# A fused linear-attention and MLP kernel: exponentials kept in head order with a GpSimd copy of their last rows, and polynomials divided by their leading coefficients

## The chip, the cores and the metric

The kernel runs on one core of a Trainium2 chip. The metric is the device time of one execution in microseconds (us). Before the change it is 695.95 us, the median of 3 runs (695.08 to 697.68). The engines are called TensorE (PE in the profile; PEld are its weight loads), VectorE (DVE), ScalarE (ACT), GpSimd (POOL) and SyncE (SP, which issues every DMA of this path).

## The reference, cut to what matters

Three parts follow one another on 3072 tokens (4 batches of 768, 8 heads of 48):

```
S_t = a_t * S_(t-1) + k_t v_t^T       a complex, |a| cut at 0.999, one factor for each of 48 rows
y_t = Re(q_t S_t)                     -> x [3072, 384]
h   = x @ w_in                        [3072, 2048]
P   = a0 + a1 h + a2 h^2 + a3 h^3
Q   = 1 + |b0| |h| + |b1| h^2
out = (P / (Q + 1e-6)) @ w_out        [3072, 384]
```

A third part (a gated set of experts) only touches tokens whose product with `w_skip` is positive.

## The kernel before, in words

**Tiling.** The 3072 tokens are 24 chunks of 128; two chunks are a unit `u`, so there are 12 units. For the attention part each chunk gets running sums over its 128 tokens, made on TensorE by a triangular matrix: of the logarithm of |a| (`mm2`, L501) and of its angle (`mm1`, L479). Two exponentials of the first sum, exp(z) into `r1` (L505) and exp(-z) into `r2` (L506), are multiplied by q and k (`qrkr`, L513) and then by cosines and sines (`prods`, L523) to give `qt` and `kt`. TensorE transposes these (`xpose`, L539), multiplies them to scores (L557), ScalarE copies the scores to `pT` (L564), GpSimd clears their upper triangle (L566), and TensorE makes y from them and from the carried state (L582, L584). The state is updated by L603 and L610 and, in chunks that are not the last of a batch, multiplied by the chunk's total decay `dec`, which is the last row (partition 127) of `r1`, moved by two small DMAs onto 96 partitions (L510).

**Layout of r1.** In the kernel before, `r1` is a view of the tile `r1t`, which holds for each token 48 rows of 8 heads: `r1t = [128, 2, 48, 8]`, `r1 = r1t.rearrange("p c d h -> p c h d")`. The row of partition 127 is then already in the order in which the DMA into `dec` wants it. Everything else that writes or reads `r1` does so by heads, with steps of 8 elements: the exponential L505, the product with q (L516, L517) and the product with the cosines (L528). `r2` lies in the order of heads, and its operations (L506, L519, L528) are otherwise the same.

**The MLP.** Each of 96 steps (12 units of 8) takes 256 of the 2048 hidden columns for 256 tokens. `G1` (L670, 18 matmuls) makes h in a PSUM tile `hb`; the weights and x are split into a high and a low part, hence three products. Then nine operations work on 128x512 elements: a1 = Square(s3 h + c), a2 = Abs(s1 h), a3 = Square(a2 + t), a4 = Ln(a3 + q0) and a5 = Exp(-a4), on ScalarE; d1 to d4 on VectorE, of which d1 and d3 make P by Horner's rule in squares and d2 and d4 refine the reciprocal. `gh` and `gl` (L701, L703) split the result, and `G2` (L714, 12 matmuls) multiplies it by w_out into `ob`. s3, s1, c, t, k, q0, p0 and sg are columns of the small tile `cf`, made once by `coefs2` (L267): square roots of |a3| and |b1| by Ln and Exp on ScalarE and one Newton step, then c, t, k and q0 from them. An activation with `scale=fine["s3"]` reads the scale from a column of `cf`, one value for each partition; a `scale` that is a number is part of the instruction.

**The order of the work.** All of this is listed as tasks with costs, and `Plan.order` (L61) simulates the engines and writes the order of each engine's instructions out once. Tasks with more than one option (for instance `gh` on VectorE or ScalarE) are placed by that simulation. `PP` (L158) holds its parameters: `NO` names options that a task may not take, `T0` and `P` give the due times of the MLP's steps, `X1`, `E0` and `E1` those of `xhi` and `xlo` (L638), which split x for G1. Each engine then runs its list strictly in order, SP's DMAs too. `late=True` tasks get their ranks by another slack.

Of the kernel before, what the change touches and what calls it, by code (L numbers as in the profile page):

```python
# [29 lines left out]
class Plan:  # L30
# [30 lines left out]
    def order(self, slack, bias, ahead, hold, cold, only):  # L61
# [93 lines left out]
        self.span = now  # L155
        self.log = out
        return [o[2] for o in out]
PP = dict(NO={'kr': ('ACT', 'POOL'), 'gl': ('ACT', 'POOL'), 'S2': ('POOL',), 'wy': ('DVE', 'POOL'), 'e4': ('ACT',), 'ev': ('DVE', 'POOL'), 'msk': ('DVE', 'POOL'), 'xabs': ('DVE',), 'cadd8': ('DVE',), 'xpe': ('DVE',), 'xlo': ('ACT', 'POOL'), 'gh': ('POOL',), 'yev': ('DVE',)}, E0=-28.045, E1=-18.577, TC=40, WS=(0, 1, 2, 3, 4, 5, 0, 1, 1, 0, 1, 2, 2, 1, 2, 2), HO={('d2b', 'ACT'): 0.925, ('msk', 'ACT'): 0, 'DVE': 0, 'POOL': 8.743}, DW=86.219, WL=9, P=6.132, LAG2=4.681, SL={'ACT': 0.3, 'DVE': 2.523, 'POOL': 0.621, 'SP': 0.41, 'PE': 3.069, '2': 2.741}, X1=25.038, T0=82.051, NZ=2, NH=3, BI={'DVE': 2.383, 'POOL': 14.689})  # L158


def main_part(tc, ctx, q, k, v, a_re, a_im, w_in, w_out, moe_a, moe_b, w_skip, out, keep):
# [15 lines left out]
    def T(name, shape, dt=F32):  # L177
        return sb.tile(shape, dt, name=name)
# [88 lines left out]
    def coefs2():  # L267

        v = nc.vector
        root, ct, p = cf[:, 0:2], cf[:, 2:4], cf[:, 6:9]
        mag, pair, half, inv, top, sq, x = (cf[:, i:i + 2] for i in (12, 14, 16, 18, 20, 22, 24))
        F = NU + 1
        v.tensor_scalar(out=abcoef.bitcast(I32), in0=ar_bc[:, 4:6].bitcast(I32), scalar1=0x7FFFFFFF,
                        scalar2=None, op0=ALU.bitwise_and)
        v.tensor_scalar(out=mag.bitcast(I32), in0=ar_bc[:, 3:6:2].bitcast(I32), scalar1=0x7FFFFFFF,
                        scalar2=None, op0=ALU.bitwise_and)
        v.reciprocal(out=x, in_=mag)
        v.tensor_scalar(out=rsum[:, F:F + 2], in0=x, scalar1=2.0 ** -60, scalar2=None, op0=ALU.mult)  # L280
        v.tensor_scalar(out=rsum[:, F + 2:F + 4], in0=mag, scalar1=2.0 ** -60, scalar2=None, op0=ALU.mult)
        v.tensor_scalar(out=mag, in0=mag, scalar1=2.0 ** -60, scalar2=2.0 ** 60, op0=ALU.max, op1=ALU.min)
# [3 lines left out]
        v.tensor_tensor(out=x, in0=mag, in1=inv, op=ALU.mult)  # L286
        v.tensor_tensor(out=x, in0=x, in1=half, op=ALU.subtract)
        v.scalar_tensor_tensor(out=root, in0=x, scalar=0.5, in1=half, op0=ALU.mult, op1=ALU.add)
        v.reciprocal(out=inv, in_=root)
        v.tensor_scalar(out=cf[:, 10:11], in0=ar_bc[:, 3:4], scalar1=0.0, scalar2=2.0, op0=ALU.is_ge, op1=ALU.mult)  # L290
        v.tensor_scalar(out=cf[:, 10:11], in0=cf[:, 10:11], scalar1=-1.0, scalar2=None, op0=ALU.add)
        v.tensor_scalar(out=fine["sg"], in0=cf[:, 10:11], scalar1=-1.0, scalar2=None, op0=ALU.mult)
        v.tensor_scalar(out=p, in0=ar_bc[:, 0:3], scalar1=cf[:, 10:11], scalar2=None, op0=ALU.mult)
        v.tensor_copy(pair[:, 0:1], cf[:, 8:9])
        v.tensor_copy(pair[:, 1:2], abcoef[:, 0:1])
        v.scalar_tensor_tensor(out=ct, in0=pair, scalar=0.5, in1=inv, op0=ALU.mult, op1=ALU.mult)
        v.tensor_tensor(out=sq, in0=ct, in1=ct, op=ALU.mult)
        v.tensor_tensor(out=fine["k"], in0=cf[:, 7:8], in1=sq[:, 0:1], op=ALU.subtract)
        v.tensor_scalar(out=fine["q0"], in0=sq[:, 1:2], scalar1=-1.0, scalar2=QEPS, op0=ALU.mult, op1=ALU.add)
        v.tensor_scalar(out=x.bitcast(I32), in0=cf[:, 6:8].bitcast(I32), scalar1=0x7FFFFFFF, scalar2=None,  # L300
                        op0=ALU.bitwise_and)
        v.tensor_tensor(out=top[:, 0:1], in0=x[:, 0:1], in1=x[:, 1:2], op=ALU.max)
        v.tensor_scalar(out=top[:, 0:1], in0=top[:, 0:1], scalar1=1e-30, scalar2=WELL, op0=ALU.max, op1=ALU.mult)
        nc.vector.memset(top[:, 1:2], WELL)
        v.reciprocal(out=top, in_=top)
        v.tensor_tensor(out=rsum[:, F + 4:F + 6], in0=sq, in1=top, op=ALU.mult)

    def lnexp():
        nc.scalar.preload_act_table_set("natural_log_exp_and_others")  # L309

    def dma(*prs):
        def f():
            for o, i in prs:
# [145 lines left out]
    def cums(u, c):  # L459
# [196 lines left out]
    def step(s):  # L656
# [511 lines left out]
```

## Time and profile before

| | |
|---|---|
| median of 3 runs | 695.95 us (695.08 to 697.68) |
| the profiled execution | 693.37 us |
| its span, first to last instruction | 691.6 us |
| mean granted TensorE clock | 0.982 |
| instructions | 12738 |

The profiled execution lies 2.6 us below the median of the three runs. Between its span and its time lie 1.8 us. Busy times of an engine are unions of its instructions' records; a matmul's record is longer than its turn in the array, since matmuls overlap.

### The profile page before, as it was taken

The page shows a single profiled execution, that of the slowest core. Times are in us where ns is not written, and L with a number is a line of the kernel's source. Part 1 is how long each engine was busy: PE and PEld are TensorE (multiplying, and loading weights), DVE is VectorE, ACT ScalarE, POOL GpSimd, SP SyncE. Part 2 cuts the span into 40 slices and gives each one's busy share as a digit, 9 for nine tenths or more (in the row PEclk, how much of TensorE's full clock was granted, in tenths as well). Part 3 has the DMA queues.
Part 4 walks back from the last instruction along what each step waited for, and adds up shares of the span by engine and source line. Part 5 has one row for each costly group of instructions (what it writes and reads, how often), then busy time and mean ns, then how long its engine had stood idle before and what let it go on. Part 6 is the DMA issues. An engine that isn't in the chain of part 4 may idle for free.

```text
span 691.6 us, 12738 instructions
## 1 busy us (share of the span) xinstructions
PE 628.6 (91%) x4772; PEld 584.3 (84%) x4772; DVE 621.1 (90%) x1020; ACT 624.9 (90%) x1022; POOL 50.9 (7%) x73
## 2 busy tenths in 40 slices
PE   0477699899999999999999999999999999999994
PEld 0154689799988999999999999999989999899993
DVE  6899999999989998988989989988998988869992
ACT  5789999999999999998999998998999989968781
POOL 2024101010010010010010010010010010000000
PEclk9999799999999999999999999999999999999997
DMA  7734333132102202202102211212112110000000
GB/s 242 260 137 144 89 101 102 50 94 84 46 22 66 60 15 72 58 16 84 47 15 73 58 27 61 58 29 71 47 38 59 49 26 17 1 11 19 13 13 29
DMA packets 52137, 43.30 MB, mean 63 GB/s; under 512 B 31200, under 2 KB 48992, under 8 KB 52064
## 3 DMA queue, kind: packets, MB, share of 16 engines
q1 hardware_dynamic: 52064, 42.38, 20.3%
q8 instruction: 39, 0.64, 0.4%
q14 instruction: 34, 0.28, 0.1%
HBM read 36.38 MB, written 4.72 MB: 59 GB/s over the span
## 4 chain that ended last, share of the span: by engine, by line
PE 47%; ACT 25%; DVE 18%; issue 5%; DMA 2%; SPq 1%; DVEq 0%; ACTq 0%
PE hb L670 15%; PE ob L714 14%; ACT wk L318 9%; PE zb L557 5%; PE zb L539 5%; DVE wk L324 3%; PE zy L582 3%; PE zb L603 2%; ACT tb L318 2%; ACT r1t L505 2%; PE zy L584 2%; DVE qt L321 1%; DVE gl L700 1%; ACT L309 1%; ACT hb L318 1%
## 5 line engine op out<-in xcount | busy, mean ns | idle before, releaser
L670 PE MATMUL hb<-xh,wih 128*128 128x256 f32 x576 | 174.0, 302 | 8.7 <-DVE wk L324 6.7
L670 PE MATMUL hb<-xl,wih 128*128 128x256 f32 x576 | 164.1, 285 | 0.4 <-DVE xl L635 0.4
L670 PE MATMUL hb<-xh,wil 128*128 128x256 f32 x576 | 163.8, 284 | 0.0
L324 DVE SCALAR_TENSOR_TENSOR wk<-wk,cf,hb 128x512 f32<-128x512 f32 x192 | 141.9, 744 | 18.0 <-ACT wk L318 8.4
L318 ACT ACTIVATE wk<-hb,cf 128x512 f32<-128x512 f32 x192 | 134.2, 733 | 20.1 <-PE hb L670 19.7
L318 ACT ACTIVATE wk<-wk,cf 128x512 f32<-128x512 f32 x192 | 139.7, 728 | 0.7
L714 PE MATMUL ob<-woh,gh 128*128 128x384 f32 x384 | 137.6, 358 | 0.0
L714 PE MATMUL ob<-wol,gh 128*128 128x384 f32 x384 | 130.4, 340 | 0.0
L714 PE MATMUL ob<-woh,gl 128*128 128x384 f32 x384 | 130.1, 339 | 0.0
L670 PEld LDWEIGHTS hb<-xh,wih 128*128 128x128 f32 x576 | 110.6, 192 | 14.2 <-DVE wk L324 7.8
L670 PEld LDWEIGHTS hb<-xl,wih 128*128 128x128 f32 x576 | 110.9, 193 | 3.6 <-DVE xl L635 1.2
L670 PEld LDWEIGHTS hb<-xh,wil 128*128 128x128 f32 x576 | 110.8, 192 | 0.0
L566 POOL TENSOR_SCALAR_AFFINE_SELECT pT<-pT 128x512 f32<-128x512 f32 x48 | 38.1, 795 | 544.4 <-ACT pT L564 544.1
L700 DVE TENSOR_TENSOR gl<-wk,gh 128x512 fp32r<-128x512 f32 x96 | 67.5, 703 | 9.3 <-ACT gh L693 4.9
L714 PEld LDWEIGHTS ob<-woh,gh 128*128 128x128 f32 x384 | 72.7, 189 | 2.8 <-issue 1.4
L714 PEld LDWEIGHTS ob<-wol,gh 128*128 128x128 f32 x384 | 72.7, 189 | 1.5
L714 PEld LDWEIGHTS ob<-woh,gl 128*128 128x128 f32 x384 | 72.5, 189 | 0.0
L324 DVE SCALAR_TENSOR_TENSOR hb<-wk,cf,hb 128x512 f32<-128x512 f32 x96 | 72.0, 750 | 0.0
L324 DVE SCALAR_TENSOR_TENSOR wk<-wk,hb 128x512 f32<-128x512 f32 x96 | 65.7, 684 | 1.2
L318 ACT ACTIVATE hb<-wk 128x512 f32<-128x512 f32 x96 | 58.0, 604 | 2.2 <-DVE wk L324 1.3
L557 PE MATMUL zb<-qT,kT 96*128 96x128 f32 x384 | 51.5, 286 | 2.0 <-ACT qT L545 0.7
L557 PEld LDWEIGHTS zb<-qT,kT 96*128 96x128 f32 x384 | 47.5, 197 | 4.1 <-ACT kT L545 1.7
(160 smaller groups left out, 1073.5 us busy)
## 6 DMA issues: line engine op xcount, KB each, us to landing
wk<-in_moe_w_in_dram SPq DMA_DIRECT2D x8, 768.0 KB
ar<-in_a_re_dram SPq DMA_DIRECT2D x24, 192.0 KB
ai<-in_a_im_dram SPq DMA_DIRECT2D x24, 192.0 KB
qraw<-in_q_dram SPq DMA_DIRECT2D x24, 192.0 KB
kraw<-in_k_dram SPq DMA_DIRECT2D x24, 192.0 KB
vb<-in_v_dram SPq DMA_DIRECT2D x24, 192.0 KB
out_dram<-x2b SPq DMA_DIRECT2D x24, 192.0 KB
xl<-in_moe_w_out_dram SPq DMA_DIRECT2D x5, 384.0 KB
```

Of the source, the lines that this page charges most:

```text
L318: return ("ACT", cost, lambda: nc.scalar.activation(out=out, in_=in_, func=func, **kw))
L324: return ("DVE", cost, lambda: nc.vector.scalar_tensor_tensor(out=out, in0=in0, scalar=scalar, in1=in1, op0=op0, op1=op1, **kw), both)
L505: nc.scalar.activation(out=r1[:, c], in_=z.rearrange("p (h d) -> p h d", h=8), func=AF.Exp)
L539: nc.tensor.transpose(z[0:96, i, :], src[:, 4 * hf + i].rearrange("p z d -> p (z d)"), ident)
L557: nc.tensor.matmul(z[:, i, :], lhsT=kT[hf][:, i, :], rhs=qT[hf][:, i, :], start=True, stop=True)
L566: pl.add([("POOL", 0.6, lambda: nc.gpsimd.affine_select(out=pT[hf], in_=pT[hf], pattern=[[0, 4], [1, 128]], base=0, channel_multiplier=-1, ...
L582: nc.tensor.matmul(dst, lhsT=vt[:, h, :], rhs=pT[hf][:, i, :], start=True, stop=first)
L584: nc.tensor.matmul(dst, lhsT=state[:, h, :], rhs=qT[hf][:, i, :], start=False, stop=True)
L603: nc.tensor.matmul(z[:, h, :], lhsT=ktc[:, h].rearrange("p z d -> p (z d)"), rhs=vt[:, h, 0:48], start=True, stop=True)
L670: nc.tensor.matmul(h[:, i * 256:i * 256 + 256], lhsT=w[:, j, fs], rhs=x[:, j, :], start=(n == 0), stop=(n == 8))
L700: eng[e].tensor_tensor(out=ghl("gl", s), in0=uu, in1=ghl("gh", s).bitcast(F32), op=ALU.subtract)
L714: nc.tensor.matmul(o, lhsT=a[:, sl], rhs=w[:, f, :], start=(f == 0 and n == 0), stop=(f == NF - 1 and n == 2))
```

## The change

The tile `r1` is now `[128, 2, 8, 48]`, in the order of heads like `r2`, and L505 writes it flat. A new tile `last` of `[128, 48, 8]` takes, by a GpSimd `tensor_copy`, the partitions 96 to 127 of `r1` in the other order, and the two DMAs into `dec` read partition 127 of `last`. There is one `last` for all chunks; 20 of the 24 chunks make the copy.

The polynomials are divided by their leading coefficients: P by a3, Q by |b1|. So a1 is Square(h + c) and a2 is Abs(h), both without a scale read from `cf`, and a2 no longer reads `cf` at all; a3, a4, a5 and d1 to d4 keep their operations. The factor a3/|b1| goes into `sg`, which multiplied the result before too. `coefs2` no longer takes square roots: it has 22 small VectorE instructions and none on ScalarE, where it had 27 (a memset among them) and 2, and it no longer waits for `lnexp`, the load of the table for Ln and Exp.

The planner's costs of the touched tasks and its parameters `PP` are changed. In `NO`, `S2` may now go to GpSimd, `whi` (the high halves of the weights) may no longer go there, and `xhi` may no longer go to VectorE. The other limits have the same effect as before.

```diff
-PP = dict(NO={..., 'S2': ('POOL',), ..., 'msk': ('DVE', 'POOL'), ...}, E0=-28.045, E1=-18.577, ..., HO={..., 'POOL': 8.743}, DW=86.219, WL=9, P=6.132, LAG2=4.681, SL={'ACT': 0.3, 'DVE': 2.523, 'POOL': 0.621, 'SP': 0.41, 'PE': 3.069, '2': 2.741}, X1=25.038, T0=82.051, ..., BI={'DVE': 2.383, 'POOL': 14.689})
+PP = dict(NO={..., 'msk': ('DVE',), 'xhi': ('DVE',), 'whi': ('POOL',)}, E0=-21.161, E1=-11.963, ..., HO={..., 'POOL': 12.521}, DW=90.883, WL=8, P=6.022, LAG2=4.584, SL={'ACT': 0.3, 'DVE': 2.523, 'POOL': 0.529, 'SP': 0.926, 'PE': 3.069, '2': 2.738}, X1=18.065, T0=86.304, ..., BI={'DVE': 5.938, 'POOL': 10.587})
-    r1t = T("r1t", [128, 2, 48, 8])
-    r1 = r1t.rearrange("p c d h -> p c h d")
+    r1 = T("r1", [128, 2, 8, 48])
+    last = T("last", [128, 48, 8])
...
+        v.tensor_copy(pair[:, 0:1], ar_bc[:, 3:4])
+        v.tensor_copy(pair[:, 1:2], abcoef[:, 1:2])
+        v.reciprocal(out=inv, in_=pair)
...
-        nc.scalar.activation(out=half, in_=mag, func=AF.Ln)
-        nc.scalar.activation(out=half, in_=half, func=AF.Exp, scale=0.5)
-        v.reciprocal(out=inv, in_=half)
...
+        v.scalar_tensor_tensor(out=fine["sg"], in0=ar_bc[:, 3:4], scalar=-1.0, in1=inv[:, 1:2], op0=ALU.mult, op1=ALU.mult)
...
-            nc.scalar.activation(out=r1[:, c], in_=z.rearrange("p (h d) -> p h d", h=8), func=AF.Exp)
+            nc.scalar.activation(out=r1[:, c].rearrange(flat), in_=z, func=AF.Exp)
...
-        pl.add([("ACT", 0.8, ex)], reads=[tl], writes=[f"r1{c}", f"r2{c}"], free=tl, name=f"exp{ci}")
+        pl.add([("ACT", 0.95, ex)], reads=[tl], writes=[f"r1{c}", f"r2{c}"], free=tl, name=f"exp{ci}")
         if ci % CPB != CPB - 1:
-            pl.add(dma(*[(dec[ci % ND][48 * z:48 * z + 48, :], r1t[127:128, c])
-                         for z in range(2)]), reads=[f"r1{c}"], writes=[("dec", ci % ND)], name=f"dec{ci}")
+            pl.add([("POOL", 0.5, lambda: nc.gpsimd.tensor_copy(last[96:128], r1[96:128, c].rearrange("p h d -> p d h")))],
+                   reads=[f"r1{c}"], writes=["last"], name="last")
+            pl.add(dma(*[(dec[ci % ND][48 * z:48 * z + 48, :], last[127:128]) for z in range(2)]), reads=["last"], writes=[("dec", ci % ND)], name=f"dec{ci}")
...
-        pl.add([act(0.66, uu, h, AF.Square, scale=fine["s3"], bias=fine["c"])], reads=hks + ["cf"], writes=[U], name="a1", late=True)
-        pl.add([act(0.57, qa, h, AF.Abs, scale=fine["s1"])], reads=hks + ["cf"], writes=[QA], name="a2", late=True)
+        pl.add([act(0.59, uu, h, AF.Square, bias=fine["c"])], reads=hks + ["cf"], writes=[U], name="a1", late=True)
+        pl.add([act(0.5, qa, h, AF.Abs)], reads=hks, writes=[QA], name="a2", late=True)
...
-    pl.add([("DVE", 3.5, coefs2)], reads=["cfr", "L"], writes=["cf"], name="cf")
+    pl.add([("DVE", 2.2, coefs2)], reads=["cfr"], writes=["cf"], name="cf")
```

## Rows read from the trace of the kernel before

**Rows 1.** Busy time by stretch: length, engines with instruction counts, granted clock, DMA share, GB/s.

```profile
0.00:100.00 100.00, 57.71 (x331) 43.64 (x332) 88.52 (x160) 84.68 (x136) 19.80 (x31) 0.93 0.50 162
100.00:200.00 100.00, 95.36 (x733) 89.25 (x731) 97.31 (x162) 98.82 (x169) 6.28 (x8) 0.98 0.24 71
200.00:620.00 420.00, 414.11 (x3299) 390.38 (x3296) 380.69 (x605) 393.74 (x644) 24.78 (x34) 1.00 0.16 44
620.00:682.00 62.00, 61.22 (x418) 60.90 (x416) 53.55 (x90) 47.63 (x76) 0.00 (x0) 1.00 0.04 16
```

**Rows 2.** Longest wait of TensorE from 100 to 620 us: total, times, longest.

```profile
PE zb L539 <- DVE qt L321: 4.0, 6, 0.8
```

**Rows 3.** Groups of operations on r1 and r2: busy us, mean ns, idle before.

```profile
L321 DVE TENSOR_TENSOR qt<-r1t,cs 128x768 f32<-128x768 f32 x24 | 38.4, 1598 | 0.1
L321 DVE TENSOR_TENSOR kt<-r,cs 128x768 f32<-128x768 f32 x24 | 22.9, 953 | 0.2 <-ACT cs L450 0.2
L321 DVE TENSOR_TENSOR r1t<-r1t,qraw 128x384 f32<-128x384 f32 x23 | 22.6, 983 | 0.4 <-DMA dec<-r1t 0.4
L321 DVE TENSOR_TENSOR r<-r,kraw 128x384 f32<-128x384 f32 x24 | 13.4, 556 | 2.5 <-ACT r L506 2.5
L505 ACT ACTIVATE r1t<-zb 128x384 f32<-128x384 f32 x24 | 22.1, 920 | 0.4 <-PE zb L501 0.4
L506 ACT ACTIVATE r<-zb 128x384 f32<-128x384 f32 x24 | 13.6, 568 | 0.0
```

**Rows 4.** Groups of ScalarE's activations out of PSUM, with and without operands from a column.

```profile
L318 ACT ACTIVATE wk<-hb,cf 128x512 f32<-128x512 f32 x192 | 134.2, 733 | 20.1 <-PE hb L670 19.7
L318 ACT ACTIVATE ys<-zy 128x512 f32<-128x512 f32 x24 | 14.3, 594 | 2.4 <-PE zy L584 2.3
L318 ACT ACTIVATE x2b<-ob,cf 128x384 f32<-128x384 f32 x24 | 13.9, 582 | 3.2 <-PE ob L714 3.2
```

**Rows 5.** Timeline of coefs2 on VectorE: its first instruction, its wait, its last.

```profile
16.00 0.16 DVE L275 TENSOR_SCALAR ab<-ar_bc 128x2 int32<-128x2 int32 x1
...
19.21 0.17 DVE L285 RECIPROCAL cf<-cf 128x2 f32<-128x2 f32 x1 [2.31 <-ACT cf L284]
...
22.33 0.16 DVE L306 TENSOR_TENSOR rsum<-cf 128x2 f32<-128x2 f32 x1
```

**Rows 6.** GpSimd: a product on r1 with two inputs.

```profile
L321 POOL TENSOR_TENSOR r1t<-r1t,qraw 128x384 f32<-128x384 f32 x1 | 1.3, 1304 | 4.0 <-ACT wk L318 4.0
```

**Rows 7.** Timeline: a pair's exponentials, the move of ys and what waits for it, a mask.

```profile
274.25 0.91 ACT L505 ACTIVATE r1t<-zb 128x384 f32<-128x384 f32 x1
275.38 0.92 ACT L505 ACTIVATE r1t<-zb 128x384 f32<-128x384 f32 x1
...
302.88 1.23 SPq L314 DMA_DIRECT2D ys<-ys  x2
...
305.50 0.55 DVE L632 CAST xh<-ys 128x384 fp32r<-128x384 f32 x1 [0.49 <-DMA ys<-ys]
...
309.97 0.63 POOL L566 TENSOR_SCALAR_AFFINE_SELECT pT<-pT 128x512 f32<-128x512 f32 x1 [9.26 <-ACT pT L564]
```

**Rows 8.** The state's product with dec: duration min/median/max in ns, first and last start.

```profile
L321 DVE TENSOR_TENSOR state<-state,dec x16: 539/548/856, 87.1 to 610.9; 96x384 f32<-96x384 f32 x16
```

**Rows 9.** VectorE's part of the high halves of x.

```profile
L632 DVE CAST xh<-ys 128x384 fp32r<-128x384 f32 x11 | 6.0, 546 | 3.3 <-DMA ys<-ys 3.3
```

**Rows 10.** Groups from 0 to 100 us.

```profile
L318 ACT ACTIVATE wk<-hb,cf 128x512 f32<-128x512 f32 x9 | 6.3, 719 | 0.0
```

**Rows 11.** Groups from 100 to 200 us.

```profile
L321 DVE TENSOR_TENSOR qt<-r1t,cs 128x768 f32<-128x768 f32 x4 | 6.5, 1618 | 0.1
L318 ACT ACTIVATE wk<-hb,cf 128x512 f32<-128x512 f32 x29 | 20.5, 735 | 0.0
```

**Rows 12.** Groups from 200 to 620 us.

```profile
L321 DVE TENSOR_TENSOR qt<-r1t,cs 128x768 f32<-128x768 f32 x16 | 25.5, 1594 | 0.0
L318 ACT ACTIVATE wk<-hb,cf 128x512 f32<-128x512 f32 x129 | 90.4, 733 | 12.0 <-PE hb L670 11.6
```

More of the change, by code (lines that the diff above doesn't have):

```diff
@@ L157, in order @@
         return [o[2] for o in out]
-PP = dict(NO={'kr': ('ACT', 'POOL'), 'gl': ('ACT', 'POOL'), 'S2': ('POOL',), 'wy': ('DVE', 'POOL'), 'e4': ('ACT',), 'ev': ('DVE', 'POOL'), 'msk': ('DVE', 'POOL'), 'xabs': ('DVE',), 'cadd8': ('DVE',), 'xpe': ('DVE',), 'xlo': ('ACT', 'POOL'), 'gh': ('POOL',), 'yev': ('DVE',)}, E0=-28.045, E1=-18.577, TC=40, WS=(0, 1, 2, 3, 4, 5, 0, 1, 1, 0, 1, 2, 2, 1, 2, 2), HO={('d2b', 'ACT'): 0.925, ('msk', 'ACT'): 0, 'DVE': 0, 'POOL': 8.743}, DW=86.219, WL=9, P=6.132, LAG2=4.681, SL={'ACT': 0.3, 'DVE': 2.523, 'POOL': 0.621, 'SP': 0.41, 'PE': 3.069, '2': 2.741}, X1=25.038, T0=82.051, NZ=2, NH=3, BI={'DVE': 2.383, 'POOL': 14.689})
+PP = dict(NO={'kr': ('ACT', 'POOL'), 'gl': ('ACT', 'POOL'), 'wy': ('DVE', 'POOL'), 'e4': ('ACT',), 'ev': ('DVE', 'POOL'), 'xabs': ('DVE',), 'cadd8': ('DVE',), 'xpe': ('DVE',), 'xlo': ('ACT', 'POOL'), 'gh': ('POOL',), 'yev': ('DVE',), 'msk': ('DVE',), 'xhi': ('DVE',), 'whi': ('POOL',)}, E0=-21.161, E1=-11.963, TC=40, WS=(0, 1, 2, 3, 4, 5, 0, 1, 1, 0, 1, 2, 2, 1, 2, 2), HO={('d2b', 'ACT'): 0, ('msk', 'ACT'): 0, 'DVE': 0, 'POOL': 12.521}, DW=90.883, WL=8, P=6.022, LAG2=4.584, SL={'ACT': 0.3, 'DVE': 2.523, 'POOL': 0.529, 'SP': 0.926, 'PE': 3.069, '2': 2.738}, X1=18.065, T0=86.304, NZ=2, NH=3, BI={'DVE': 5.938, 'POOL': 10.587})
 def main_part(tc, ctx, q, k, v, a_re, a_im, w_in, w_out, moe_a, moe_b, w_skip, out, keep):
@@ L189, in main_part @@
     amin, rsum = keep["amin"], keep["rsum"]
-    cf = cp.tile([128, 40], F32, name="cf")
-    fine = {n: cf[:, i:i + 1] for n, i in (("s3", 0), ("s1", 1), ("c", 2), ("t", 3), ("k", 4), ("q0", 5), ("p0", 6), ("sg", 9))}
+    cf = cp.tile([128, 18], F32, name="cf")
+    fine = {n: cf[:, i:i + 1] for n, i in (("c", 0), ("t", 1), ("p0", 2), ("k", 3), ("q0", 4), ("sg", 5))}
     tri = cp.tile([128, 128], F32, name="tri")
@@ L271, in coefs2 @@
         v = nc.vector
-        root, ct, p = cf[:, 0:2], cf[:, 2:4], cf[:, 6:9]
-        mag, pair, half, inv, top, sq, x = (cf[:, i:i + 2] for i in (12, 14, 16, 18, 20, 22, 24))
+        ct, p = cf[:, 0:2], cf[:, 2:4]
+        pair, inv, sq, top, x = (cf[:, i:i + 2] for i in (8, 10, 12, 14, 16))
         F = NU + 1
[L275 to L278, printed above, removed]
@@ L279, in coefs2 @@
-        v.reciprocal(out=x, in_=mag)
-        v.tensor_scalar(out=rsum[:, F:F + 2], in0=x, scalar1=2.0 ** -60, scalar2=None, op0=ALU.mult)
-        v.tensor_scalar(out=rsum[:, F + 2:F + 4], in0=mag, scalar1=2.0 ** -60, scalar2=None, op0=ALU.mult)
-        v.tensor_scalar(out=mag, in0=mag, scalar1=2.0 ** -60, scalar2=2.0 ** 60, op0=ALU.max, op1=ALU.min)
-        nc.scalar.activation(out=half, in_=mag, func=AF.Ln)
-        nc.scalar.activation(out=half, in_=half, func=AF.Exp, scale=0.5)
-        v.reciprocal(out=inv, in_=half)
@@ L286, in coefs2 @@
[L286 to L296, printed above, removed]
+        def mag(out, in_):
+            v.tensor_scalar(out=out.bitcast(I32), in0=in_.bitcast(I32), scalar1=0x7FFFFFFF, scalar2=None,
+                            op0=ALU.bitwise_and)
+        mag(abcoef, ar_bc[:, 4:6])
@@ new lines, in coefs2 @@
+        mag(x, ar_bc[:, 3:6:2])
+        v.tensor_scalar(out=rsum[:, F + 2:F + 4], in0=x, scalar1=2.0 ** -60, scalar2=None, op0=ALU.mult)
+        v.tensor_copy(pair[:, 0:1], ar_bc[:, 3:4])
+        v.tensor_copy(pair[:, 1:2], abcoef[:, 1:2])
+        v.reciprocal(out=inv, in_=pair)
+        mag(x, inv)
+        v.tensor_scalar(out=rsum[:, F:F + 2], in0=x, scalar1=2.0 ** -60, scalar2=None, op0=ALU.mult)
+        v.tensor_tensor(out=pair[:, 0:1], in0=ar_bc[:, 2:3], in1=inv[:, 0:1], op=ALU.mult)
@@ L297, in coefs2 @@
+        v.tensor_tensor(out=pair[:, 1:2], in0=abcoef[:, 0:1], in1=inv[:, 1:2], op=ALU.mult)
+        v.tensor_scalar(out=ct, in0=pair, scalar1=0.5, scalar2=None, op0=ALU.mult)
         v.tensor_tensor(out=sq, in0=ct, in1=ct, op=ALU.mult)
[L298 to L301, printed above, removed]
+        v.tensor_scalar(out=p, in0=ar_bc[:, 0:2], scalar1=inv[:, 0:1], scalar2=None, op0=ALU.mult)
@@ L302, in coefs2 @@
+        mag(x, p)
         v.tensor_tensor(out=top[:, 0:1], in0=x[:, 0:1], in1=x[:, 1:2], op=ALU.max)
-        v.tensor_scalar(out=top[:, 0:1], in0=top[:, 0:1], scalar1=1e-30, scalar2=WELL, op0=ALU.max, op1=ALU.mult)
-        nc.vector.memset(top[:, 1:2], WELL)
+        mag(top[:, 1:2], inv[:, 1:2])
+        v.tensor_scalar(out=top, in0=top, scalar1=1e-30, scalar2=WELL, op0=ALU.max, op1=ALU.mult)
         v.reciprocal(out=top, in_=top)
         v.tensor_tensor(out=rsum[:, F + 4:F + 6], in0=sq, in1=top, op=ALU.mult)
+        v.tensor_tensor(out=fine["k"], in0=p[:, 1:2], in1=sq[:, 0:1], op=ALU.subtract)
@@ L308, in lnexp @@
+        v.scalar_tensor_tensor(out=fine["q0"], in0=inv[:, 1:2], scalar=QEPS, in1=sq[:, 1:2], op0=ALU.mult,
+                               op1=ALU.subtract)
+        v.scalar_tensor_tensor(out=fine["sg"], in0=ar_bc[:, 3:4], scalar=-1.0, in1=inv[:, 1:2], op0=ALU.mult, op1=ALU.mult)
     def lnexp():
@@ L515, in qrkr @@
             hs = slice(8 * c, 8 * c + 8)
-            pl.add([tt("POOL", 1.13, r1[:, c], r1[:, c], raw["q"][:, hs, :], ALU.mult),
+            pl.add([tt("POOL", 0.96, r1[:, c], r1[:, c], raw["q"][:, hs, :], ALU.mult),
                     tt("DVE", 0.47, r1[:, c], r1[:, c], raw["q"][:, hs, :], ALU.mult)],
@@ L527, in prods @@
             i0 = r[:, c].unsqueeze(2).to_broadcast([128, 8, 2, 48])
-            pl.add([tt("DVE", 0.87, t, i0, csl, ALU.mult), tt("POOL", 2.12 if nm == "r1" else 1.76, t, i0, csl, ALU.mult)],
+            pl.add([tt("DVE", 0.87, t, i0, csl, ALU.mult), tt("POOL", 1.76, t, i0, csl, ALU.mult)],
                    reads=[f"{nm}{c}", f"cs{c}"], writes=[key], name="pr" + nm)
@@ L678, in step @@
         QA, U, R = ("qa", s % 3), ("u", s % 3), ("r", s % 2)
-        pl.add([act(0.66, uu, h, AF.Square, scale=fine["s3"], bias=fine["c"])], reads=hks + ["cf"], writes=[U], name="a1", late=True)
-        pl.add([act(0.57, qa, h, AF.Abs, scale=fine["s1"])], reads=hks + ["cf"], writes=[QA], name="a2", late=True)
-        pl.add([act(0.6, qa, qa, AF.Square, bias=fine["t"])], reads=["cf"], writes=[QA], name="a3", late=True)
+        pl.add([act(0.59, uu, h, AF.Square, bias=fine["c"])], reads=hks + ["cf"], writes=[U], name="a1", late=True)
+        pl.add([act(0.5, qa, h, AF.Abs)], reads=hks, writes=[QA], name="a2", late=True)
+        pl.add([act(0.63, qa, qa, AF.Square, bias=fine["t"])], reads=["cf"], writes=[QA], name="a3", late=True)
         pl.add([stt(0.66, uu, uu, fine["k"], h, ALU.add, ALU.mult, both=False)], reads=hks + ["cf"], writes=[U], name="d1", late=True)
-        pl.add([act(0.6, r, qa, AF.Ln, bias=fine["q0"])], reads=[QA, "cf"], writes=[R], name="a4", late=True)
+        pl.add([act(0.63, r, qa, AF.Ln, bias=fine["q0"])], reads=[QA, "cf"], writes=[R], name="a4", late=True)
         pl.add([act(0.52, h, r, AF.Exp, scale=-1.0)], reads=[R], writes=hks, name="a5", late=True)
```

## The prediction

> **What bounds the kernel now.** I read the busy times by stretch first. There are four stages [rows 1]. From 0 to 100 us the start has TensorE busy for only 57.7 us; VectorE (88.5) and ScalarE (84.7) load, split weights and run the first chunks, and TensorE waits for them. From 100 to 200 us both of these are full (97.3 and 98.8), TensorE at 95.4. From 200 to 620 us the three are close together, TensorE 414.1 of 420, ScalarE 393.7, VectorE 380.7. From 620 us on only the MLP is left, and TensorE is busy 61.2 of 62 us. TensorE's recorded idle time is thus 42.3, 4.6, 5.9 and 0.8 us in the stages. The records flatter it, since matmuls overlap and a gap inside a record's length doesn't show. So VectorE and ScalarE set the pace up to 200 us, TensorE does mostly after that, and nothing that they lose after 620 us counts.
>
> Then the waits of TensorE: from 100 to 620 us the longest sum is that of the transposes for `qt`, the product of r1 with the cosines on VectorE, 4.0 us in six waits [rows 2]. The change touches exactly that producer.
>
> Then the groups by shape, for prices. The three operations on `r1` have each a twin on `r2` of the same shape in head order [rows 3]: 1598 against 953 ns, 983 against 556, 920 against 568.
>
> **Step 1, r1 in head order.** I take the twins as the new prices. VectorE: 24 products with the cosines lose 0.645 us each, 15.5 us; 23 products with q lose 0.427 us each, 9.8 us. ScalarE: 24 exponentials lose 0.352 us each, 8.4 us. Bounds: nothing, if the steps were not what costs; but input, shape and engine are the same in each pair, and only the order differs, so I take the whole.
>
> **Step 2, no scale from a column.** a1 and a2 average 733 ns; the copy of the same shape out of PSUM with no such operand takes 594 [rows 4]. The two hold three column operands together (two scales, one bias), 1.5 on average, so one costs 139/1.5 = 93 ns. Bounds: 14 ns, from the 384 wide copy with a scale (582, [rows 4]) against the exponential without one (568, [rows 3]), and 139 ns if the bias is free. I take 93, as it comes from the very operations: 192 x 0.093 = 17.8 us of ScalarE. a3, a4, a5 and d1 to d4 are unchanged.
>
> **Step 3, coefs2.** It holds VectorE from 16.00 to 22.49 us, 2.3 us of that waiting for two activations, which stand behind a table load in ScalarE's queue [rows 5]. The wait goes, and 5 of 27 instructions at about 0.16 us: 3.1 us of VectorE, in the start. Since a2 no longer reads `cf` and the chain has no turn on ScalarE, nothing new waits for it.
>
> **Step 4, the copy on GpSimd.** 20 new instructions of 384 elements, one input, read in steps of 48 elements. No such copy is in the trace. Bounds: 1.3 us, from the product on GpSimd with two inputs, one of them strided [rows 6], and 0.5 us, from a mask's 0.63 us for 512 elements in a row [rows 7]. I take 0.9. GpSimd is busy for 25 of 420 us [rows 1], so its time is free in itself. The chain exponential, copy, two DMAs, `dec` grows by about 1 us, and the state's product reads `dec` only after the transposes and the update of its chunk, which cover it; without that cover it would cost VectorE's queue 1 us a chunk. In return the product with q waits for the copy instead of the DMA's read.
>
> It costs VectorE something: the state's product takes 548 ns in the median but up to 856 [rows 8], the slow one under the mask at 309.97 us [rows 7]. For a copy I take 0.2 us of VectorE, between 0 (no overlap) and 0.9 (the whole copy): 20 x 0.2 = 4 us.
>
> [...]
>
> **Step 5, what the planner moves.** `xhi` may no longer go to VectorE: 11 casts of 0.546 us [rows 9] leave VectorE and come to ScalarE, 6 us each way. `gh` can go to either, so the two even out; I price it at nothing in the sum. If they could not be evened, ScalarE would keep 6 us of its 26. The state's second product may go to GpSimd, where a two-input product took 1.3 us against 0.55 [rows 6, 8]; that is 9 us of VectorE for nothing, if it happens, with the same contention. `xhi` is also due some 7 us later ahead of its G1 (`X1`), which is cover taken away: a late `xl` would stop the whole of G1. I leave both out of the sum and let them widen the range.
>
> **The sum, stage by stage.** The gains are laid where the instructions are; of the cosine products 4 lie from 100 to 200 us [rows 11], 16 from 200 to 620 [rows 12], so 4 before.
>
> 0 to 100 us: VectorE 4 x 0.645 + 4 x 0.427 + 3.1 = 7.4; ScalarE 4 x 0.352 + 9 x 0.093 = 2.2, with 9 of a1 and a2 there [rows 10]. The chain changes between the two, and VectorE is the fuller. I take 4.5, near the middle.
>
> 100 to 200 us: VectorE 4 x 1.072 = 4.3; ScalarE 4 x 0.352 + 29 x 0.093 = 4.1 [rows 11]. Both are full, so it shortens by 4.2.
>
> 200 to 620 us: VectorE 16 x 1.072 = 17.2; ScalarE 16 x 0.352 + 129 x 0.093 = 17.6 [rows 12]. These are not the bound. What can be had is TensorE's waiting: between 0 and 17.4 (if the stage followed the two engines one for one), with 5.9 us of recorded idle time as the nearest row. I take 4.0, about the waits for `qt`.
>
> After 620 us: nothing.
>
> Added: of 20 x 0.2 us some 7 copies fall before 200 us, 1.4 us whole; of the other 2.6 the share that the third stage passes on, 4.0/17.4, is 0.6. Together 2.0.
>
> 4.5 + 4.2 + 4.0 - 2.0 = 10.7 us. The profiled execution took 693.37 us (span 691.6 and 1.8 around it), so 682.7; it lies 2.6 us below the median of the three runs, and so I predict 685.3, 1.5% faster.
>
> **Rivals.** First, TensorE is the bound throughout and the start hangs on ScalarE: the third stage gives 0, the start 2.2, the second stage half of its 4.2, less 2.0 for contention, so 2.3 us: 693.7, no change that can be told. For it: 95.4 and 414.1 us busy [rows 1]. Against it: records hide gaps, and `qt` is the first wait.
>
> Second, more than forecast: the third stage passes on two thirds of 17.4, 11.6 us, and the start 6: 4.2 + 11.6 + 6 - 3 = 18.8, so 677. For it: ScalarE at 94% and VectorE at 91% with a chain of nine operations that changes between them; against it the 5.9 us of idle time.
>
> Third, contention at full length: 20 x 0.9 = 18 us of VectorE. Before 200 us 6.3 of it eats most of the 8.7, and the third stage's 17.2 shrink to 5.5, of which 1.3 passes: 3.7 us gained, 692.3, the edge of no change.
>
> Fourth, slower: `last` is a single tile. The second copy of a pair waits until the first one's DMAs have read it. The exponentials of a pair start 1.1 us apart, and a like pair of DMAs took 2.6 us from issue to use [rows 7]. GpSimd's list is in order, so a mask behind the waiting copy waits too, and behind that y; SP's list is in order as well, and the loads and the move of ys stand behind the second pair of DMAs; the product with q waits for the copy. 8 pairs are both copied, so up to 8 x 2.6 = 21 us: 685.3 + 21 = 706. It decides for slower when more than 14.2 us of it is exposed (the gain of 10.7 and the 3.5 below), 1.8 us a pair. Against it: GpSimd is busy 6% of that stage [rows 1], so few masks can stand right behind a copy.
>
> **How the numbers follow.** About 0.5%, 3.5 us, is what a measurement of this kernel can tell from no change. Forecast 0.60 and second rival 0.14 are faster; first 0.10 and third 0.05 are the same, the third half over the edge; the fourth is slower, 0.11. So 0.74, 0.15, 0.11. The range reaches down to the second rival and up to the first: 677 to 694.
>
> **What would show it.** In the profile after: `qt` at about 950 ns, r1 with q at 556, the exponential at 568, a1 and a2 at about 640 on average; coefs2 some 4 us long with no wait; VectorE's busy time near 595 and ScalarE's near 600; 100 to 200 us with more matmuls than 733 [rows 1]; the waits for `qt` shorter. It is wrong if copies wait on DMAs, masks wait behind copies, or G1 waits for `xl`; or if TensorE's idle time from 200 us on is as before, when only the start has given anything.

## The result

| | median | runs | profiled execution | its span |
|---|---|---|---|---|
| before | 696.5 us | 695.08 to 697.68 | 693.37 us | 691.6 us |
| after | 680.43 us | 679.61 to 680.69 | 679.61 us | 677.7 us |

The changed kernel is 2.3% faster: ratio 0.9768, 95% interval 0.9747 to 0.979. (The 696.5 us before is the median of four runs, one more than the 695.95 us above.) That is 16.1 us between the medians, and 13.8 us between the two profiled executions, where 10.7 us had been forecast.

The busy times by stretch of the kernel after, to be laid beside [rows 1] (length, then PE, PEld, DVE, ACT and POOL with their counts, granted clock, DMA share, GB/s):

```profile
0.00:100.00 100.00, 58.65 (x382) 46.42 (x383) 90.86 (x165) 87.99 (x144) 21.37 (x34) 0.88 0.51 164
100.00:200.00 100.00, 96.54 (x743) 90.19 (x741) 96.63 (x163) 96.40 (x171) 8.44 (x11) 0.98 0.24 70
200.00:620.00 420.00, 419.09 (x3332) 399.66 (x3331) 372.15 (x613) 384.74 (x659) 36.45 (x47) 1.00 0.16 45
620.00:682.00 62.00, 47.04 (x322) 46.64 (x320) 41.99 (x73) 33.00 (x54) 0.00 (x0) 0.93 0.05 15
```

Read the counts of matmuls first, since the same 4772 are done in both kernels: 51 more by 100 us, 10 more in the second stage, 33 more in the third. VectorE and ScalarE do more instructions there in less busy time, and TensorE has next to no recorded idle time left in the third stage (0.9 us, from 5.9).

The groups that answer to [rows 3] and [rows 4], and the copy (busy us, mean ns, idle before):

```profile
L316 DVE TENSOR_TENSOR qt<-r,cs 128x768 f32<-128x768 f32 x24 | 22.8, 949 | 1.1 <-PE zb L535 1.0
L316 DVE TENSOR_TENSOR r<-r,qraw 128x384 f32<-128x384 f32 x24 | 13.9, 582 | 0.7 <-POOL last L505 0.7
L316 DVE TENSOR_TENSOR r<-r,kraw 128x384 f32<-128x384 f32 x24 | 16.2, 674 | 1.2 <-ACT r L501 1.2
L500 ACT ACTIVATE r<-zb 128x384 f32<-128x384 f32 x24 | 11.8, 491 | 1.0 <-PE zb L496 0.6
L501 ACT ACTIVATE r<-zb 128x384 f32<-128x384 f32 x24 | 11.9, 497 | 0.0
L313 ACT ACTIVATE wk<-hb,cf 128x512 f32<-128x512 f32 x96 | 66.0, 687 | 0.9 <-DVE gl L696 0.8
L313 ACT ACTIVATE wk<-hb 128x512 f32<-128x512 f32 x96 | 57.3, 597 | 24.4 <-PE hb L666 24.1
L505 POOL COPY last<-r 32x384 f32<-32x384 f32 x20 | 24.1, 1207 | 246.9 <-ACT r L500 209.1 <-issue 22.0 <-DMA dec<-last 10.1
```

The products with the cosines now cost what their twin cost. The product with k, which the change doesn't touch, rose from 556 to 674 ns. Both exponentials are shorter, also the second one, which had head order all along. The copies waited 10.1 us for DMAs in all.

Last, the waits of TensorE from 100 to 620 us, in answer to [rows 2]:

```profile
PE zb L599 <- ACT r L501: 1.2, 1, 1.2
PE zb L496 <- DVE xr L487: 1.1, 1, 1.1
```

These are the two longest; the wait for `qt`, 4.0 us before, is gone from the list.

**Where the time came from.** G1 has 1728 matmuls in 96 steps of 18, in the same sequence in every kernel here, so the start of a given step can be compared. Step 24 begins at these rows of the timeline, before and then after:

```profile
229.73 0.28 PE L670 MATMUL hb<-xh,wih 128*128 128x256 f32 x1
```

```profile
222.60 0.28 PE L666 MATMUL hb<-xh,wih 128*128 128x256 f32 x1
```

So the first two stages gave 7.1 us in these two executions. From there to the last matmul of G1 it is 440.6 us before and 433.6 after, another 7.0; what lies behind that is 0.2 us longer. The busy times between these two matmuls, before and after (columns as above):

```profile
229.73:670.33 440.60, 434.81 (x3420) 413.40 (x3420) 401.22 (x638) 406.69 (x660) 23.51 (x32) 1.00 0.14 40
222.60:656.16 433.56, 432.65 (x3421) 414.58 (x3421) 385.54 (x634) 390.38 (x664) 34.28 (x44) 1.00 0.15 41
```

TensorE does the same work in both; its weight loads take 413.4 and 414.6 us for it. VectorE is busy for 15.7 us less and ScalarE for 16.3.

The same count for all kernels follows (us; the difference to the kernel before in brackets). It is one execution of each. The first column of times varies with the execution as well: the granted clock from 0 to 100 us is 0.93 in the profile before and 0.88 after. From 200 to 620 us it is 1.00 in both.

| kernel | ratio, 95% | step 24 begins | from there to G1's end |
|---|---|---|---|
| before | 1 | 229.7 | 440.6 |
| after | 0.9768 [0.9747, 0.979] | 222.6 (-7.1) | 433.6 (-7.0) |
| o4_coefs | 0.9956 [0.994, 0.9973] | 227.6 (-2.1) | 440.8 (+0.2) |
| o1_polys | 0.9905 [0.9868, 0.9943] | 227.0 (-2.7) | 437.9 (-2.7) |
| o2_layout | 0.985 [0.982, 0.9881] | 226.8 (-2.9) | 433.6 (-7.0) |
| o3_both | 0.9771 [0.9741, 0.9801] | 227.5 (-2.2) | 433.2 (-7.4) |
| n3_oldboth | 0.9961 [0.9945, 0.9977] | 228.0 (-1.7) | 440.9 (+0.3) |
| n1_oldlayout | 0.9897 [0.9873, 0.992] | 225.8 (-3.9) | 439.2 (-1.4) |
| n2_oldscale | 0.983 [0.9814, 0.9846] | 225.0 (-4.7) | 437.1 (-3.5) |
| n4_copytwice | 0.9913 [0.9896, 0.9929] | 226.9 (-2.8) | 437.1 (-3.5) |
| n6_idlecopy | 0.986 [0.9839, 0.988] | 226.6 (-3.1) | 435.6 (-5.0) |
| n5_twolast | 0.9771 [0.9753, 0.9789] | 221.5 (-8.2) | 433.1 (-7.5) |
| n7_flatcopy | 0.9744 [0.9727, 0.9761] | 222.1 (-7.7) | 433.2 (-7.4) |
| p1_P | 0.9853 [0.9824, 0.9883] | 226.6 (-3.2) | 431.4 (-9.2) |

One per cent of the ratio is 7.0 us; below, prices in us are ratios times 696.

### The profile page after: what moved, and what is told of

The parts are those of the page before. It is cut to its first block, busy times and chain, and to the rows that moved or that the text cites. A ratio compares the mean times of both kernels' runs of the same rounds, so it can differ in the third digit from the quotient of the medians.

```text
span 677.7 us, 12769 instructions
## 1 busy us (share of the span) xinstructions
PE 621.3 (92%) x4772; PEld 582.9 (86%) x4772; DVE 601.6 (89%) x1011; ACT 602.1 (89%) x1025; POOL 66.3 (10%) x92
## 4 chain that ended last, share of the span: by engine, by line
PE 75%; DVE 10%; ACT 7%; DMA 3%; issue 2%; SPq 1%; POOL 0%; ACTq 0%; DVEq 0%; POOLq 0%
PE hb L666 27%; PE ob L710 25%; PE zb L553 6%; PE zb L535 5%; PE zy L578 3%; PE zb L599 3%; DVE wk L319 2%; PE zb L474 2%; PE zy L580 2%; PE zb L496 2%; ACT wk L313 2%; SPq L309 1%; DMA xl<-in_moe_w_out_dram 1%; DVE gl L696 1%; DMA ys<-ys 1%
## 5 line engine op out<-in xcount | busy, mean ns | idle before, releaser
L313 ACT ACTIVATE wk<-hb 128x512 f32<-128x512 f32 x96 | 57.3, 597 | 24.4 <-PE hb L666 24.1
L313 ACT ACTIVATE wk<-hb,cf 128x512 f32<-128x512 f32 x96 | 66.0, 687 | 0.9 <-DVE gl L696 0.8
L562 POOL TENSOR_SCALAR_AFFINE_SELECT pT<-pT 128x512 f32<-128x512 f32 x48 | 34.7, 726 | 281.4 <-ACT pT L560 280.6
```

The source lines that it names most:

```text
L562: pl.add([("POOL", 0.6, lambda: nc.gpsimd.affine_select(out=pT[hf], in_=pT[hf], pattern=[[0, 4], [1, 128]], base=0, channel_multiplier=-1, ...
```

## The experiments

The theory of the prediction, called loads: VectorE and ScalarE have less to do, and so the pace rises. Its first rival, order: the planner's new costs and parameters drew a better order of the lists, and the cheaper instructions matter little. The o kernels keep the order of the kernel before and take the new instructions; the n kernels keep the order of the kernel after and take some old instructions back, or change the copy. Of a long changed line, the diffs here show the call alone.

**o1_polys and o4_coefs: the polynomials.** o1 has the new coefs2 and a1 and a2 without a scale from a column; o4 has the new coefs2 alone, since its a1 and a2 read a column of ones. The difference of the two:

```diff
-act(0.66, uu, h, AF.Square, bias=fine["c"])
-act(0.57, qa, h, AF.Abs)
+act(0.66, uu, h, AF.Square, scale=keep["one"], bias=fine["c"])
+act(0.57, qa, h, AF.Abs, scale=keep["one"])
```

> The order of every engine's work is that of the kernel before; only the polynomials are divided by their leading coefficients (a1 and a2 without a scale from a column, the short coefs2); r1 keeps its old layout and there is no copy. Loads theory (what counts is that the engines have less to do): ScalarE loses 17.8 us and VectorE 3.1 us; with one of the two full engines eased, about 5 to 6 us are gained, 691. Order theory (what counts is that the planner, with truer costs and other parameters, wrote a better order): within 2 us of the kernel before, 695 to 698.

> The order of the kernel before, r1 in its old layout, a1 and a2 with a scale column of ones; only the short coefs2 without ScalarE is new. By the prediction's third step the start loses 3.1 us of VectorE: 693.5, with the first G1 some 2 us earlier. If the start doesn't hang on it, 696. With dividing the polynomials and all at 688.7, the rest would be the scale operands' share.

Measured: o1 688.65 us (687.68 to 691.57), o4 692.77 us. The new coefs2 alone gives 0.44%, 3.1 us, and all of it lies ahead of step 24. The scales then give 0.5%, 3.5 us, of which 2.9 in the third stage; the two intervals just overlap, and n2 below settles that the scales gain.

**o2_layout: head order and the copy alone**, in the order of before; the copy is issued right ahead of its DMAs.

```diff
-    r1t = T("r1t", [128, 2, 48, 8])
-    r1 = r1t.rearrange("p c d h -> p c h d")
+    r1 = T("r1", [128, 2, 8, 48])
+    last = T("last", [128, 48, 8])
...
+            def copy_and_move():
+                nc.gpsimd.tensor_copy(last[96:128], r1[96:128, c].rearrange("p h d -> p d h"))
+                f_()
...
```

> The order of the kernel before, polynomials as before; only r1 lies in the order of heads, with the GpSimd copy issued right before its two DMAs. Loads theory: VectorE loses 25 us less some 4 of contention, ScalarE 8.4; about 6 us are gained, 690.5. Order theory: within 2 us of the kernel before.

Measured: 685.56 us, 1.5%, 10.4 us: the larger part of the change, and 7.0 of it in the third stage. The prices fit that: it takes 25 us from VectorE and 8 from ScalarE, the scales only 18 from ScalarE.

**o3_both and n3_oldboth: order against loads.** o3 has every new instruction in the order of before; n3 has the order of after, with the old layout and the columns of ones, so only coefs2 and the copies are new in it; its copies read and write in a row.

```diff
-    r1 = T("r1", [128, 2, 8, 48])
+    r1t = T("r1t", [128, 2, 48, 8])
+    r1 = r1t.rearrange("p c d h -> p c h d")
...
-act(0.59, uu, h, AF.Square, bias=fine["c"])
+act(0.59, uu, h, AF.Square, scale=keep["one"], bias=fine["c"])
```

> The order of the kernel before with all of the new instructions, polynomials and layout and copy. Loads theory: the predicted 10.7 us, 685.8, and what is left to the changed kernel (some 5 us) belongs to the new order. Order theory: within 3 us of the kernel before, 693.5 to 698.

> The order of the changed kernel with the old prices: r1 in the old layout (the copy to last stays, now with a read in a row), and a1 and a2 with a scale column of ones. coefs2 stays short. Loads theory: the gain is lost but for what the new order and coefs2 give, 690 to 694. Order theory: within 3 us of the changed kernel, 680 to 684.

Measured: o3 681.48 us, ratio 0.9771 beside the 0.9768 of the change; n3 693.18 us, 0.9961 beside the 0.9956 of o4. So with every new instruction the two orders come out within 0.05% of each other, with intervals of 0.2 to 0.3% each way. With the old ones they do as well, but that pair is less clean: n3 makes 20 copies that o4 doesn't. The VectorE instructions that overlap them in n3's trace exceed their medians by 1.5 us in all, so the order could hide about that much there. The order theory falls. What the new `PP` moved between engines is chiefly the 11 casts of `xh`, from VectorE to ScalarE, and 6 casts of `gh` the other way; `S2` and the masks, though `NO` changed for them, run where they ran before. None of this, nor `X1`, brings anything that these runs can tell.

**n1_oldlayout and n2_oldscale: one part taken back** in the order of after, by the first and the second half of n3's edit.

> The order of the changed kernel, new polynomials, but r1 in the old layout: cosine products, products with q and the first exponential at their old prices (25 us of VectorE, 8.4 of ScalarE); the copy to last reads in a row. Loads theory: about half of the gain goes, 686 to 689. Order theory: 680 to 683.

> The order of the changed kernel, new layout, but a1 and a2 read a scale of ones from a column: 192 x 0.093 = 17.8 us more for ScalarE. Loads theory: about 5 us of the gain go, 685 to 687. Order theory: 680 to 682. If the price of a column operand is nearer to 14 ns than to 93, no change under either.

Measured: n1 688.51 us, so the layout is worth 1.29%, 9.0 us, with its stepped copy in place of n1's copy in a row; n2 684.17 us, so the scales are worth 0.62%, 4.3 us. Coefs2 (3.1), the scales (2.4 to 4.5, by the pair of kernels that is compared) and the layout (9.0 to 10.4) add up to 14.5 to 18.0 us around the 16.1 measured: the parts add, as far as intervals of 0.2 to 0.4% each way can tell. How a part's gain lies over the stages changes with the order: the new layout with the old scales has 7.0 us of it in the third stage in o2 and 3.5 in n2.

The groups of n2 show the price of a column operand. Beside a1 and a2 of the kernel after, 687 and 597 ns, it is 94 and 93 ns, where 93 had been worked out:

```profile
L313 ACT ACTIVATE wk<-hb,cf,one 128x512 f32<-128x512 f32 x96 | 75.0, 781 | 0.9 <-DVE gl L696 0.8
L313 ACT ACTIVATE wk<-hb,one 128x512 f32<-128x512 f32 x96 | 66.2, 690 | 18.4 <-PE hb L666 18.2
```

**n4_copytwice and n6_idlecopy: the price of a copy.** n4 makes each copy to `last` twice. n6 adds a second copy that reads `last` and writes a tile that nothing reads, so nobody waits for it. Neither takes or adds anything else. n6's edit:

```diff
+    idle = T("idle", [128, 8, 48])
...
+nc.gpsimd.tensor_copy(idle[96:128], last[96:128].rearrange("p d h -> p h d"))
```

> The changed kernel with every copy to last made twice: 20 more copies of 0.9 to 1.2 us on GpSimd. By the prediction's term (0.2 us of VectorE for a copy, half of it passed on) 1 to 2 us slower; by the contention rival (each copy stops VectorE for its whole length) 5 us or more; if copies cost nothing, within 0.5 us of the changed kernel.

> The changed kernel, same order, with a second copy behind each copy to last that reads last (in steps, for as long as the first) and writes a tile that nobody reads, so that the product with q doesn't wait for it. With the copies doubled it was 9 us slower, of which 6 us were waits of the product with q and some 4 us longer instructions of VectorE. If the waiting was what cost: within 2 us of the changed kernel, 680 to 683. If sharing with GpSimd was what cost: most of the 9 us stay, 686 to 690. If both count as they stand in VectorE's records: 683 to 686.

Measured: n4 689.51 us and n6 685.91 us, 10.1 and 6.4 us above the kernel after, 0.50 and 0.32 us for each of the 20 extra copies. A copy on an engine that is busy 66.3 us of the span is thus not free, even if nobody waits for it; in n6 TensorE doesn't wait longer for masks either (0.8 us in all, 1.6 in the kernel after). The first part of n6's page says where it is paid, in VectorE's busy time (DVE; 601.6 us in the kernel after):

```profile
PE 623.5 (91%) x4772; PEld 583.3 (85%) x4772; DVE 609.0 (89%) x1011; ACT 602.4 (88%) x1025; POOL 94.3 (14%) x112
```

VectorE is busy for 7.4 us more, and the end comes 6.4 us later. These second copies are longer than the first ones (1285 against 904 ns in the median; GpSimd is busy for 94.3 us in place of 66.3), so this isn't yet the price of the copies that the change made. By stage, with the row to be laid beside the two from step 24 on:

```profile
226.65:662.25 435.60, 433.83 (x3421) 414.43 (x3420) 389.12 (x634) 390.36 (x664) 51.20 (x56) 1.00 0.15 41
```

From step 24 on VectorE has 3.6 us more and 2.0 us are lost; ahead of it, 3.8 us more and 4.0 lost. In n4 the product with q waits as well, by its list of waits (0.7 us in the kernel after):

```profile
DVE r L316 <- POOL last L505: 6.7, 6, 2.5
```

The timeline of the kernel after shows how VectorE pays (start, us, engine, operation):

```profile
122.30 0.83 POOL L505 COPY last<-r 32x384 f32<-32x384 f32 x1 [17.54 <-ACT r L500]
122.38 1.57 DVE L319 SCALAR_TENSOR_TENSOR tb<-ar,tb 128x768 f32<-128x768 f32 x1
...
176.08 0.74 DVE L319 SCALAR_TENSOR_TENSOR wk<-wk,cf,hb 128x512 f32<-128x512 f32 x1
176.33 0.88 POOL L505 COPY last<-r 32x384 f32<-32x384 f32 x1 [24.05 <-ACT r L500]
...
223.02 0.98 POOL L505 COPY last<-r 32x384 f32<-32x384 f32 x1 [2.54 <-DMA dec<-last]
223.15 1.66 DVE L316 TENSOR_TENSOR ai<-ai,tb 128x768 f32<-128x768 f32 x1
...
374.81 1.46 POOL L505 COPY last<-r 32x384 f32<-32x384 f32 x1 [2.52 <-DMA dec<-last]
375.44 1.12 DVE L691 CAST gh<-wk 128x512 fp32r<-128x512 f32 x1
```

`ai<-ai,tb` and `tb<-ar,tb` take 0.95 us in the median; begun 0.1 us after a copy they took 0.71 and 0.62 us more, where the copies had 0.85 and 0.75 us left to run. The cast, 0.42 us in the median, took 1.12, 0.70 more, with 0.83 us of its copy left. The Horner step `wk<-wk,cf,hb`, which has `hb` from PSUM, never took more than 0.75 us in 192 instances, copies above it or not. Adding up, for all 20 copies, how far the VectorE instructions that overlap them exceed their medians gives 6.4 us, 0.32 a copy.

**n5_twolast: two tiles in turns**, for the fourth rival.

```diff
-    last = T("last", [128, 48, 8])
+    lasts = [T(f"last{i}", [128, 48, 8]) for i in range(2)]
...
```

> The changed kernel, same order, with two tiles last in turns, so that the second copy of a pair doesn't wait for the first one's DMAs. By the fourth rival's mechanism, if it costs anything, 2 us or more are gained; if the wait is covered, within 1 us of the changed kernel.

Measured: 679.33 us, 0.9771 beside 0.9768. GpSimd's wait for the DMAs that read `last` falls to half, by its lists of waits in the kernel after and in n5, and nothing comes of it:

```profile
POOL last L505 <- DMA dec<-last: 10.1, 4, 2.6
```

```profile
POOL last L506 <- DMA dec<-last: 4.8, 2, 2.4
```

**n7_flatcopy: a copy in a row.** It reads and writes `last` without a change of order; the decays so come to `dec` in another order.

```diff
-nc.gpsimd.tensor_copy(last[96:128], r1[96:128, c].rearrange("p h d -> p d h"))
+nc.gpsimd.tensor_copy(last[96:128].rearrange("p d h -> p (d h)"), r1[96:128, c].rearrange("p h d -> p (h d)"))
```

> The changed kernel, same order, with a copy to last that reads and writes in a row, so that the decays reach the state in another order than the reference's; all else is the same work. GpSimd's copy should fall from 1.2 to some 0.6 us. If the stepped read is what makes the copy dear to VectorE, 2 to 4 us faster than the changed kernel, 676 to 678; if it is the copy as such or nothing, within 1 us.

Measured: 678.3 us, 0.9744; its interval overlaps that of the change, so a gain of some 1.7 us is likely and not settled. The copy and the product with k, in its groups:

```profile
L505 POOL COPY last<-r 32x384 f32<-32x384 f32 x20 | 17.2, 862 | 250.0 <-ACT r L500 214.5 <-issue 22.0 <-ACT tb L313 5.0
L316 DVE TENSOR_TENSOR r<-r,kraw 128x384 f32<-128x384 f32 x24 | 13.6, 565 | 1.2 <-ACT r L501 1.2
```

With a mean of 862 ns in place of 1207 for the copy (505 against 898 in the median), the product with k is back at 565 ns. That it had been lengthened by the stepped copies is the reading of these rows, and the timeline agrees: in the kernel after, the products with k that began 0.2 and 0.5 us behind the start of a copy took up to 0.69 us more than their median. VectorE's busy time falls by 4.0 us, to 597.6, and some 1.7 us came of it.

**p1_P: the planner's sensitivity.** `P` goes from 6.022 to 6.06, nothing else.

```diff
-DW=90.883, WL=8, P=6.022, LAG2=4.584
+DW=90.883, WL=8, P=6.06, LAG2=4.584
```

> The changed kernel with one planner parameter moved a little, P from 6.022 to 6.06, which changes the order of the work in many places and no instruction's price. If the order is a fine balance, the time moves by several us, 683 to 690; if orders of this planner are alike, within 2 us of the changed kernel.

Measured: 685.07 us (681.49 to 687.35), 0.9853, which is 5.9 us slower than the change, for a parameter moved by 0.6%. The profiled execution is the fastest of the four, 3.6 us below their median: in it the third stage is the best of all (431.4 us) and step 24 begins 4.0 us later than in the kernel after. Where the rest of the 5.9 us lies, no trace shows. So a draw of the order can cost as much as a part of the change, although the two orders of this case happen to be equal.

A version without any copy was not tried, so what the 20 copies themselves cost the end is bounded only loosely, by n6 and n7. No version here is clearly faster than the changed kernel.

## Why the prediction was right

The sign, the mechanism and the range held; the time of 685.3 us was 4.9 too high. Against its own profiled execution the sum said 682.7 and the profile gave 679.6, 3.1 us more of a gain.

**Step 1 (head order), right.** `qt` at 949 ns against 953 forecast, the product with q at 582 against 556. The exponential fell further than its twin had said, to 491 instead of 568 ns, because the twin itself was lengthened (last section). That is 0.07 us for each of the 48 exponentials, 3.6 us of ScalarE that the sum left out. All 24 products with q now run on VectorE, where 23 were priced.

**Step 2 (scales), right:** 94 and 93 ns against 93. The lower bound of 14 ns was built on the lengthened twin (568 ns); against the 497 ns that it takes after the change, the same pair would have said 85. ScalarE's busy time is 602.1 us, forecast near 600.

**Step 3 (coefs2), right:** first and last instruction in the kernel after:

```profile
15.98 0.16 DVE L277 TENSOR_SCALAR ab<-ar_bc 128x2 int32<-128x2 int32 x1
...
18.91 0.15 DVE L301 SCALAR_TENSOR_TENSOR cf<-ar_bc,cf 128x1 f32<-128x1 f32 x1
```

It holds VectorE for 3.1 us, with no wait, where it held it for 6.5 and waited behind a table load of ScalarE that took 1.28 us (at 17.45 us in the timeline of the kernel before); 3.1 us less were forecast (the "some 4 us long" among the signs doesn't follow from that sum), 3.4 are measured. At the end it is worth 3.1 us (o4), by the profiles all of it ahead of step 24.

**Step 5 (the planner), rightly left out:** o3 beside the changed kernel. The casts of `xh` left VectorE, 6.0 us, and those of `gh` brought 4.9 back; the state's product stayed on VectorE.

**First two stages.** Forecast 4.5 + 4.2, less 1.4 for copies, 7.3; the two profiles show 7.1, counted to step 24, which begins 30 us behind the end of the forecast's second stage. That agreement is worth less than it looks: o3, with the same instructions, shows 2.2 in an execution that is 2.5 us above its median and has a granted clock of 0.80 from 0 to 100 us. If the third stage gives 7.0 in each, the 16.1 us between the medians leave some 9 for the first two.

**The failed step: the term of the third stage, mis-sized.** "I take 4.0, about the waits for `qt`", with 5.9 us of recorded idle time as the nearest row; less 0.6 for copies, 3.4. Measured from step 24 on: 7.0 us, and 7.4 and 7.5 in o3 and n5, at a clock of 1.00. VectorE lost 15.7 us there and ScalarE 16.3, copies included, so something under half was passed on (0.43 to 0.45) and not a quarter. The text had the reason itself: matmuls overlap, so that a gap inside a record's length doesn't show (in both timelines the first matmuls of step 24 begin 0.12 us apart, with records of 0.28 us). Then recorded idle time understates what can be had, and it was used as the middle. A better row was in the same line of [rows 1]: weight loads busy 390.4 of 420 us, 29.6 us free. Over the same work, from step 24 on, the loads stay at 413.4 and 414.6 us while the recorded matmul time shrinks from 434.8 to 432.6: beside the loads 27.2 us are free before and 19.0 after, beside the matmuls 5.8 and 0.9, less than the 7.0 gained.

**Step 4 (the copy), mis-sized the other way.** The copy takes 898 ns in the median, 0.9 forecast. But VectorE pays 0.32 us a copy, not 0.2: 6.4 us where the sum had 4. What the end pays is bounded less well. n6's longer copies put 7.4 us on VectorE and 6.4 on the end; n7 took 4.0 from VectorE and gave 1.7, not clear of noise. The sum's 2.0 is thus likely to be too low, and by how much stays open. If it is, the two errors partly cancel, and the gain that the copies are set against was larger than measured. VectorE's total (601.6 us, forecast near 595) contains this contention.

**The rivals.** First, TensorE bound: fallen, o1 and o2 gain in the third stage. Second, more than forecast (677): its third stage passed on two thirds, the forecast's a quarter; the measured share lies between the two, and so does the result. Third, contention at full length: fallen in size (0.32 of 0.9 us), true in kind. Fourth, one `last`: the waits exist, 10.1 us, and are covered (n5). That copies wait on DMAs had been named as a sign of being wrong; by itself it wasn't one.

The extra load of n6 passed on in much the same way as the relief: 2.0 of 3.6 us from step 24 on, and 4.0 beside 3.8 us ahead of it, where the prediction had found VectorE and ScalarE full. The part ahead of step 24 is less sure, as the clock from 0 to 100 us was 0.97 in n6 and 0.88 in the kernel after. What stays open: why it is about half in the third stage. With ScalarE alone relieved it was less: in o1 ScalarE lost 10.9 us from step 24 on (406.7 to 395.8), VectorE 0.9, and 2.7 came of it.

## What to carry to other kernels

Where three engines are nearly full and TensorE's recorded idle time is small, don't cap a gain by that idle time: look at the room beside the weight loads as well (here 5.8 us idle, 27.2 beside the loads, 7.0 gained). Here a little under half of what the two feeding engines lost was passed on, a quarter when ScalarE alone was relieved. An operand's order in memory cost two thirds more here (1598 against 949 ns for the same product), and moving the reorder to 32 rows on a mostly idle engine paid even after contention (10.4 us in o2). Price work on GpSimd by what it puts on VectorE, here 0.32 us for each copy of 0.90, not by GpSimd's own busy share, here 10%.

## What the runs showed of the hardware

Behind a strided exponential the next one took longer. With the old layout (n1) the pair takes 922 and 564 ns; in head order 491 and 497, although the second instruction is the same in both:

```profile
L501 ACT ACTIVATE r1t<-zb 128x384 f32<-128x384 f32 x24 | 22.1, 922 | 1.1 <-PE zb L497 1.0
L502 ACT ACTIVATE r<-zb 128x384 f32<-128x384 f32 x24 | 13.5, 564 | 0.0
```

So the layout freed ScalarE of 12 us and not of the 8.4 that was forecast.

A GpSimd copy may also have been the one that was held up. The third copy of the kernel after began inside a run of two-input instructions of VectorE, and took 4.49 us, five times the median of 0.90; that they held it up is the reading of the timeline, and no run tests it:

```profile
62.37 4.49 POOL L505 COPY last<-r 32x384 f32<-32x384 f32 x1 [4.71 <-ACT r L500]
62.49 0.94 DVE L344 SCALAR_TENSOR_TENSOR wk<-wk 128x768 int32<-128x768 int32 x1
```
